# Dealing rows to partitions in consecutive blocks in a hash-attention and feed-forward kernel

## The chip, the cores and the metric

The kernel runs on one core of a Trainium2 chip. The metric is device time in microseconds (us) of the whole program; lower is better. The core has the matrix engine TensorE (PE in the profile, its weight loads PEld), VectorE (DVE), ScalarE (ACT), GpSimd (POOL) and SyncE (SP), which here only issues DMAs. SBUF and PSUM, the on-chip memories, have 128 partitions.

## The reference

Two operations follow each other. The first is attention in which a query sees only the keys whose hash bucket is its own: six sign bits of a projection make the bucket.

```python
B, H, S, D = 4, 8, 768, 64
q_bits = (np.einsum('bhsd,dk->bhsk', q, proj) > 0)      # proj: 64 x 6
k_bits = (np.einsum('bhsd,dk->bhsk', k, proj) > 0)
mask = q_bucket[:, :, :, None] == k_bucket[:, :, None, :]
scores = np.where(mask, np.matmul(q, k.transpose(0, 1, 3, 2)) / 8, -1e9)
attn = softmax(scores)                                  # with 1e-9 added to the sum
x = (attn @ v).transpose(0, 2, 1, 3).reshape(B, S, 512)
# the second: layer norm without a bias, and a feed-forward layer added to x
xn = (x - x.mean(-1)) / np.sqrt(x.var(-1) + 1e-6) * g_ln
out = x + np.maximum(xn @ w_ch1, 0.0) @ w_ch2           # 512 -> 2048 -> 512
```

Inputs and output are float32. The kernel multiplies in bfloat16, the hash bits aside, which come from float32 matmuls.

## The kernel before

**Tiling.** The work is cut into 12 units u: batch b = u // 3, and a third of the query rows, 256 of 768, in two tiles of 128. A unit has six steps s, two groups g of four heads by three key pieces kp of 256 keys. Step s computes transposed scores (`scores`, L182), their exponential (`exps`, L189, ScalarE), and one step later the product with v (`av`, L206). After three steps `normalize` (L219 to L223) divides by the row sums and collects statistics; after six `center` (L230 to L233) subtracts the mean, and `flip` (L238) transposes the result by DMA. Then come `ff1` (L248, relu at L252 into `hb`), `ff2` (L258, residual at L265 into `res`) and `store` (L272), spread over the following unit's steps.

**How rows sit on partitions.** The 768 rows of a head are tt = 32 blocks of 24 neighbouring rows; a block is c = 4 times kj = 6 rows. q and k of four heads are loaded with (head, tt) on the partitions, so a partition holds 24 neighbouring rows of one head. VectorE then transposes blocks of 32x32, which puts a row's 64 features on the partitions (two halves j of 32) and tt in the free dimension. `turn` (L78 to L83, batches 1 to 3, three kj at a time) and `first_piece` (L282 to L288, batch 0, two kj at a time) lay the columns out in the order (kj, c, tt): the 32 values of a block are neighbours in memory. A matmul over 128 columns then takes one kj, and its partition is p = 32 c + tt. For that v must have the same order: partition 32 c + tt takes the rows 24 tt + 6 c to 24 tt + 6 c + 5. One DRAM view holds this for only one c, so `load_v` (L145) issues four DMAs of 32 partitions per half of the heads, and `store` (L272) four per unit.

**Hash.** For batch 0, `first` transposes one piece, casts it, multiplies by the projection (L301) and takes the signs (`bits`, L86) into G, one piece after another. For batches 1 to 3, `turn_piece` (four per tensor and group, 16 per batch), `cast_full` (GpSimd, L97 and L113), `hash_mm` (L123) and `bits` (L86) do the same in larger pieces; then `hash_move` (L133) issues 16 small DMAs per group.

**Order.** Every piece of work is an event with a key in units of steps, and the program is emitted in the order of the keys; each engine works through its own list in that order. q and k of the next batch are transposed in the seven steps ahead of their first use (S0 = 18 b + 3 g):

```python
at(S0 - 7 + 1.3 * t + 0.3 * n, turn_piece, b, g, t, n)
at(S0 - 5.7 + 1.3 * t, cast_full, b, g, t)
at(S0 - 4.2, hash_mm, b, g)
at(S0 - 3.9 + 0.1 * (4 * c + i), hash_move, b, g, c, i)
at(S0 - 9, load_v, b, 0)
at(6 * u + 6.12, flip, u)
```

Nearly all DMAs are issued by SyncE (q, k, v, w_ch1, hash moves, flips, stores), so that its list is one queue: a flip stands behind the hash moves and stores with smaller keys. Buffers shared by name tag set further waits: three for X (the loaded q and k), two for `big` (v and the pieces of w_ch1 in turn), one PSUM buffer each for `f1`, `f2`, `acc` and `sc`. In batch 0 the pieces of w_ch1 are cast on VectorE (`cast_w1`, L316) between the pieces of `first`, and the v sums (`sum_v`, L164 to L166) are taken on GpSimd.

Of the kernel before, what the change touches and what calls it, by code (L numbers as in the profile page):

```python
# [15 lines left out]
def kernel(  # L16
# [15 lines left out]
    nc = tc.nc  # L32
    P = 128
    B, H, S, D = q.shape
# [5 lines left out]
    KJ, CC, TT = 6, 4, 32  # L40
# [9 lines left out]
    def qk_view(t, b, g):  # L50
        return t[b, 4 * g : 4 * g + 4].rearrange("i (tt r) d -> (i tt) (r d)", tt=TT)

    v_view = [v[b].rearrange("h (tt c kj) d -> c tt h (kj d)", tt=TT, c=CC) for b in range(B)]
    out_view = [out[b].rearrange("(tt c u qt) d -> u c tt (qt d)", tt=TT, c=CC, u=3) for b in range(B)]
    w1ap = moe_w_ch1.rearrange("(o p) h -> p o h", p=P)
    w2ap = moe_w_ch2.rearrange("(o p) d -> p o d", p=P)

# [16 lines left out]
    X, T, vnat = {}, {}, {}  # L74
    sc, E, acc = {}, {}, {}
    xt, stats, rstd, xc, xnT, hb, f2, res = {}, {}, {}, {}, {}, {}, {}, {}


    def turn(dst, src, j, kj0, n):

        s = src.rearrange("p (c kj j dd) -> p j kj c dd", c=CC, j=2, dd=32)
        d = dst.rearrange("p j (kj c t) -> p j kj c t", c=CC, t=32)
        nc.vector.transpose(d[:, j, kj0 : kj0 + n], s[:, j, kj0 : kj0 + n])  # L83

    def bits(dst, src):
# [7 lines left out]
    def cast_q(eng, b, g, src, lo, hi):  # L93
        if eng is nc.scalar:
            nc.scalar.activation(qb[b, g][:, :, lo:hi], src, AF.Copy, scale=QS)
        else:
            eng.tensor_scalar(qb[b, g][:, :, lo:hi], src, QS, None, op0=AOP.mult)  # L97
# [5 lines left out]
    def turn_piece(b, g, t, n):  # L103
        if n == 0:
            T[b, g, t] = pool.tile([P, 2, S], F32, name=f"T{b}{g}{t}", tag="T", bufs=2)
        j, half = n // 2, n % 2
        turn(T[b, g, t], X[b, g, t], j, 3 * half, 3)
# [31 lines left out]
    def load_v(b, hs):  # L139
        if hs == 0:  # L140
            vnat[b] = pool.tile([P, H, KJ * D], F32, name=f"vnat{b}", tag="big", bufs=2)
            vaug[b] = pool.tile([P, H, KJ, D + 1], BF16, name=f"vaug{b}", tag="vaug", bufs=2)
            vsum[b] = pool.tile([P, H, D + 1], BF16, name=f"vsum{b}", tag="vsum", bufs=2)
        for c in range(CC):
            nc.sync.dma_start(  # L145
                out=vnat[b][32 * c : 32 * c + 32, hs : hs + 4],
                in_=v_view[b][c][:, hs : hs + 4],
            )

    def cast_v(b, hs, n):  # L150
        nc.gpsimd.tensor_copy(
# [116 lines left out]
            )  # L268

    def store(u):  # L270
        for c in range(CC):
            nc.sync.dma_start(  # L272
                out=out_view[u // 3][u % 3][c],
                in_=res[u][32 * c : 32 * c + 32].rearrange("p t d -> p (t d)"),
            )


    def x_piece(b, g, t, kp, tag, bufs, eng):
# [4 lines left out]
    def first_piece(b, g, t, kp, tag, bufs, caster):  # L283
        tp = pool.tile([P, 2, 256], F32, name=f"T{b}{g}{t}{kp}", tag=tag, bufs=bufs)
        for j in range(2):
            s = X[b, g, t, kp].rearrange("p c (kj j dd) -> p j kj c dd", j=2, dd=32)
            d = tp.rearrange("p j (kj c t) -> p j kj c t", c=CC, t=32)
            nc.vector.transpose(d[:, j], s[:, j])  # L288
        lo, hi = 256 * kp, 256 * kp + 256
        if t == 0:  # L290
            cast_q(caster, b, g, tp, lo, hi)
        elif caster is nc.scalar:
            nc.scalar.copy(kb[b, g][:, :, lo:hi], tp)
        else:
            caster.tensor_copy(kb[b, g][:, :, lo:hi], tp)
        return tp
# [7 lines left out]
    def first(g, t, kp, xtag, ttag, caster, bank):  # L304
        tp = first_piece(0, g, t, kp, ttag[0], ttag[1], caster)
        first_hash(0, g, t, kp, tp, bank)
# [20 lines left out]
    def start_loads():  # L327
        nc.vector.memset(pfull, 0.0)
        nc.vector.memset(warm, 0.25)
        x_piece(0, 0, 0, 0, *XP, nc.sync)  # L330
        x_piece(0, 0, 1, 0, *KX, nc.sync)
        for i in range(4):
            nc.scalar.dma_start(
                out=pfull[32 * i : 32 * i + 32, :, 32 * i : 32 * i + NB],
                in_=proj.rearrange("(j dd) n -> dd j n", j=2),
            )
        nc.scalar.dma_start(out=g_sb, in_=moe_g_ln.rearrange("(o p) -> p o", p=P))
        nc.vector.memset(bias_sb, EXP_BIAS)
        nc.gpsimd.memset(p32, 0.0)
        nc.gpsimd.memset(mhalf, -0.5)  # L340
        nc.gpsimd.memset(epsm, EPS_ROW)
        for kp in (1, 2):
            x_piece(0, 0, 1, kp, *KX, nc.sync)
        load_v(0, 0)
        for i in range(4):
            nc.gpsimd.tensor_copy(
                p32[32 * i : 32 * i + 32, :, 8 * i : 8 * i + NB],
                pfull[32 * i : 32 * i + 32, :, 32 * i : 32 * i + NB],
            )
# [16 lines left out]
    for kp in range(3):  # L366
        at(-0.5 + 0.1 * kp, x_piece, 0, 1, 1, kp, *KX, nc.sync)
    at(-0.3, load_v, 0, 4)
    at(-0.2, cast_v, 0, 0, 4)
    at(0.6, sum_v, 0, 0, 4)  # L370
# [23 lines left out]
    for b in range(1, B):  # L394
        for g in range(2):
            S0 = 18 * b + 3 * g
            at(S0 - 10, load_x, b, g, 0)
            at(S0 - 9.5, load_x, b, g, 1)
            at(S0 - 7.2, new_group, b, g)
            for t in range(2):  # L400
                for n in range(4):
# [3 lines that stand above are left out]
            for c in range(4):  # L405
                for i in range(4):
                    at(S0 - 3.9 + 0.1 * (4 * c + i), hash_move, b, g, c, i)
        S0 = 18 * b
        at(S0 - 9, load_v, b, 0)
        at(S0 - 8.8, load_v, b, 4)  # L410
        at(S0 - 5, ones_v, b)
        for hs in range(0, 8, 2):
            at(S0 - 5 + 0.5 * hs / 2 + (2.6 if hs > 3 else 0), cast_v, b, hs, 2)
        for hs in (0, 4):
            at(S0 - 3.2 + 2.6 * hs / 4, sum_v, b, hs, 4)
# [22 lines left out]
    for u in range(NU):  # L438
        for p in range(4):
            ff(ff1, u, p, "f1" if u or p % 2 == 0 else "f2")  # L440
            if u:
                key = ff(ff2, u - 1, 1, p, "f2")
                if p == 3:
                    at(key + 0.3, store, u - 1)
            else:
                chunk[0] += 1
        ff(ff1, u, 4, "f1")
        ff(ff1, u, 5, "f2")
        ff(ff1, u, 6, "f1")
        ff(ff2, u, 0, 0, "f2")  # L450
        ff(ff1, u, 7, "f1")
        for p in range(1, 4):
            ff(ff2, u, 0, p, "f2")
    for p in range(4):
        key = ff(ff2, NU - 1, 1, p, "f1")
    at(key + 0.3, store, NU - 1)

    with tc.manual_schedule():
# [32 lines left out]
```

The softmax here doesn't subtract the row's maximum and nothing guards it: scores larger than these inputs give would overflow.

## Time and profile before

| | us |
|---|---|
| runs of the kernel before, median of three | 366.18 |
| lowest and highest | 364.65, 366.58 |
| span of the profiled execution, first to last instruction | 363.9 |
| first unit's preparation, until the feed-forward begins | about 64 |

The profiled execution has no recorded time of its own beside its span. What a run's time has beyond the span lies ahead of the first and behind the last instruction.

| operation | count | mean us | busy us |
|---|---|---|---|
| block transpose L288, 128x256 f32, VectorE | 24 | 0.419 | 9.1 |
| block transpose L83, 128x384 f32, VectorE | 48 | 0.555 | 25.4 |
| relu L252, VectorE | 96 | 0.683 | 65.6 |
| hash matmul L301, 128x256 f32, TensorE | 48 | 0.514 | 18.1 |
| v load L145, issue on SyncE, 192 KB each | 32 | 0.436 (median) | |
| store L272, issue on SyncE, 128 KB each | 48 | 0.418 (median) | |
| hash move L133, issue on SyncE | 96 | 0.721 (median) | |

A pair or run of transposes overlaps a little: in the start two of them take 0.76 us together, and in a run of L83 they begin 0.48 us apart.

In the profile's rows a line number is one of the listing above. A row of waits gives who waited for whom, the sum in us, how often, and the longest. A row of the chain gives a start time, a length, and the engine with its work; the chain runs back from the last instruction of the program through whatever released each step. A row of engines gives busy us, share of the span and number of instructions. The rows of digits cut the span into 40 slices and give tenths of busy time.

### The profile page before, as it was taken

What the parts mean: (1) busy time and instruction counts of PE and PEld (TensorE: products, weight loads), DVE (VectorE), ACT (ScalarE), POOL (GpSimd) and SP (SyncE); (2) the same over time, 40 slices, a digit from 0 to 9 for tenths busy, and PEclk for the clock granted to TensorE, in tenths of its full rate; (3) what the DMA queues carried; (4) which work ended last, traced back from release to release, by engine and by line L of the source; (5) the groups of instructions that cost most, each with busy time, mean ns of one, the idle gap of its engine ahead of it and who ended that gap; (6) DMA issues with size and microseconds to landing.
All of it is one profiled execution on the core that took longest, in us unless ns stands there. A gap on an engine that the chain in (4) does not pass through costs nothing.

```text
span 363.9 us, 9678 instructions
## 1 busy us (share of the span) xinstructions
PE 312.7 (86%) x4281; PEld 209.8 (58%) x4344; DVE 183.3 (50%) x373; ACT 144.7 (40%) x76; POOL 100.5 (28%) x106
## 2 busy tenths in 40 slices
PE   8674457989988989989989989898889899897993
PEld 3353335766665666756656657666656567565561
DVE  1427245385662363578444534955624545446341
ACT  2344204662453554445246445533535455442000
POOL 1656142019940010069710010399200100101000
PEclk9989555899999999999999999999999999999899
DMA  7799931991021039860030279700210302203022
GB/s 170 174 243 212 306 112 29 273 260 23 9 64 34 3 88 278 193 141 7 12 78 13 59 204 242 192 7 8 64 35 2 88 2 59 31 2 78 10 59 58
DMA packets 34873, 35.68 MB, mean 98 GB/s; under 512 B 17424, under 2 KB 29712, under 8 KB 34832
## 3 DMA queue, kind: packets, MB, share of 16 engines
q1 hardware_dynamic: 31872, 32.96, 36.0%
q0 software_dynamic: 2112, 2.10, 3.6%
q8 instruction: 34, 0.56, 0.6%
q10 hardware_dynamic: 848, 0.01, 0.2%
q14 instruction: 7, 0.06, 0.1%
HBM read 27.27 MB, written 6.29 MB: 92 GB/s over the span
## 4 chain that ended last, share of the span: by engine, by line
PE 66%; DVE 15%; SPq 5%; DMA 4%; issue 3%; ACT 3%; POOL 1%; ACTq 0%; DVEq 0%; POOLq 0%
PE f L248 19%; PE f L258 18%; PE sc L182 11%; PE acc L206 8%; PE hf L301 4%; SPq L133 4%; DVE hb L252 3%; ACT E L189 3%; PE hp L123 2%; DVE xc L231 2%; DMA w1f<-in_moe_w_ch_dram 2%; DMA xnT<-xc 2%; PE warm L354 2%; DVE x L221 2%; DVE st L223 1%
## 5 line engine op out<-in xcount | busy, mean ns | idle before, releaser
L189 ACT ACTIVATE E<-sc,bias_sb 128x2048 bf16<-128x2048 f32 x72 | 141.6, 1967 | 173.9 <-PE sc L182 173.9
L248 PE MATMUL f<-xnT,w_sb 128*128 128x256 bf16 x768 | 99.7, 274 | 16.3 <-DVE hb L252 13.8
L248 PEld LDWEIGHTS <-w_sb 128*128 128x128 bf16 x768 | 72.4, 98 | 39.1 <-issue 23.0
L252 DVE TENSOR_SCALAR hb<-f 128x512 bf16<-128x512 f32 x96 | 65.6, 683 | 52.7 <-PE f L248 51.4
L258 PE MATMUL f<-w_sb,hb 128*128 128x512 bf16 x321 | 86.9, 385 | 3.5
L232 POOL TENSOR_SCALAR rs<-mv 128x2 f32<-128x2 f32 x12 | 6.1, 512 | 199.6 <-DVE mv L230 199.6
L182 PE MATMUL sc<-qb,kb 32*128 32x256 bf16 x1152 | 54.2, 275 | 0.0
L258 PEld LDWEIGHTS <-hb 128*128 128x128 bf16 x384 | 35.2, 99 | 30.5 <-issue 3.2
L206 PEld LDWEIGHTS <-E 128*128 128x128 bf16 x1152 | 43.1, 100 | 11.4 <-issue 10.5
L206 PE MATMUL acc<-vaug,E 128*128 128x65 bf16 x1152 | 49.5, 198 | 0.0
L265 DVE SCALAR_TENSOR_TENSOR res<-f,rs,x 128x512 f32<-128x512 f32 x24 | 18.0, 751 | 54.7 <-PE f L258 50.7
L182 PE MATMUL sc<-G 6*128 6x256 bf16 x576 | 41.9, 280 | 4.0 <-ACT E L189 3.9
L97 POOL TENSOR_SCALAR qb<-T 128x1536 bf16<-128x1536 f32 (+1 forms) x10 | 30.6, 3059 | 13.4 <-DVE T L288 13.4
L182 PEld LDWEIGHTS <-G 6*128 6x128 bf16 x576 | 15.4, 92 | 29.7 <-issue 28.6
L182 PEld LDWEIGHTS <-kb 32*128 32x128 bf16 x1152 | 30.8, 96 | 2.0
L301 PE MATMUL hf<-T,pfull 128*128 128x256 f32 x48 | 18.1, 514 | 13.6 <-DVE T L288 13.5
L83 DVE STREAM_TRANSPOSE T<-X 128x384 f32<-128x384 f32 x48 | 25.4, 555 | 0.0
L301 PEld LDWEIGHTS hf<-T,pfull 128*128 128x128 f32 x48 | 10.7, 246 | 18.7 <-DVE T L288 17.2
L223 DVE BATCH_NORM_STATS2 st<-x 128x6 f32<-128x256 f32 x48 | 18.1, 418 | 0.8
L221 DVE TENSOR_TENSOR x<-acc,rc 128x512 f32<-128x512 f32 x24 | 16.6, 692 | 0.8
L86 DVE TENSOR_SCALAR G<-hf 128x256 bf16<-128x256 f32 x12 | 5.1, 425 | 23.5 <-PE hf L301 23.5
L219 DVE RECIPROCAL rc<-acc 128x8 f32<-128x8 f32 x24 | 4.9, 205 | 21.1 <-PE acc L206 21.1
(35 smaller groups left out, 147.9 us busy)
## 6 DMA issues: line engine op xcount, KB each, us to landing
vnat<-in_v_dram SPq DMA_DIRECT2D x32, 192.0 KB
out_dram<-res SPq DMA_DIRECT2D x48, 128.0 KB
X<-in_q_dram SPq DMA_DIRECT2D x6, 768.0 KB
X<-in_k_dram SPq DMA_DIRECT2D x6, 768.0 KB
w1f<-in_moe_w_ch_dram SPq DMA_DIRECT2D x4, 1024.0 KB
w_sb<-in_moe_w_ch_dram POOLq DMA_DIRECT2D x4, 512.0 KB, 8.5
X<-in_q_dram SPq DMA_DIRECT2D x6, 256.0 KB
X<-in_k_dram SPq DMA_DIRECT2D x6, 256.0 KB
```

Source lines behind the costliest of these rows:

```text
L83: nc.vector.transpose(d[:, j, kj0 : kj0 + n], s[:, j, kj0 : kj0 + n])
L97: eng.tensor_scalar(qb[b, g][:, :, lo:hi], src, QS, None, op0=AOP.mult)
L182: nc.tensor.matmul(sc[s][:, i, 256 * kk : 256 * kk + 256], lh, rh, start=(rep == 0), stop=(rep == 2), skip_group_check=True,)
L189: nc.scalar.activation(E[s], sc[s], AF.Exp, scale=EXP_SCALE, bias=bias_sb)
L206: nc.tensor.matmul(acc[u, g][:, qt, (D + 1) * i : (D + 1) * (i + 1)], E[s][:, i, 256 * kk + P * qt : 256 * kk + P * qt + P], vaug[u // 3][ ...
L221: nc.vector.tensor_tensor(xo, a[:, :, :, 0:D], rc.to_broadcast([P, 2, 4, D]), op=AOP.mult)
L223: nc.vector.bn_stats(stats[u][:, qt, g], xt[u][:, qt, 256 * g : 256 * g + 256])
L248: nc.tensor.matmul(f1[:, n].rearrange("p (t x) -> p t x", t=2), w1_sb[:, dt, P * nt : P * nt + P], xnT[u][:, :, dt], start=(dt == 0), stop ...
L252: nc.vector.tensor_scalar_max(hb[u][:, 2 * p : 2 * p + 2], f1, 0.0)
L258: nc.tensor.matmul(f2[u, t], hb[u][:, nt, P * t : P * t + P], w2_sb[:, nt], start=(nt == 0), stop=(nt == NNT - 1),)
L265: nc.vector.scalar_tensor_tensor(res[u][:, t], f2[u, t], rstd[u][:, t : t + 1], xt[u][:, t], op0=AOP.mult, op1=AOP.add,)
L301: nc.tensor.matmul(hp[:, :256], pfull[:, j], tp[:, j], start=(j == 0), stop=(j == 1))
```

## The change

Partition p now takes the rows 6 p to 6 p + 5, that is p = 4 tt + c where it was 32 c + tt. v and the output then have one regular view over all 128 partitions, and the four DMAs become one. The transposes of q and k have to deliver their columns in the same order, (kj, tt, c): the 32 values of a block are written four elements (16 bytes) apart, and the four blocks of one kj interleave. Nothing else is edited; the readers of the transposed tiles still read them without gaps.

```diff
-    v_view = [v[b].rearrange("h (tt c kj) d -> c tt h (kj d)", tt=TT, c=CC) for b in range(B)]
-    out_view = [out[b].rearrange("(tt c u qt) d -> u c tt (qt d)", tt=TT, c=CC, u=3) for b in range(B)]
+    v_view = [v[b].rearrange("h (p kj) d -> p h (kj d)", p=P) for b in range(B)]
+    out_view = [out[b].rearrange("(p u qt) d -> u p (qt d)", p=P, u=3) for b in range(B)]
...
     def turn(dst, src, j, kj0, n):
 
         s = src.rearrange("p (c kj j dd) -> p j kj c dd", c=CC, j=2, dd=32)
-        d = dst.rearrange("p j (kj c t) -> p j kj c t", c=CC, t=32)
+        d = dst.rearrange("p j (kj t c) -> p j kj c t", c=CC, t=32)
         nc.vector.transpose(d[:, j, kj0 : kj0 + n], s[:, j, kj0 : kj0 + n])
...
-        for c in range(CC):
-            nc.sync.dma_start(
-                out=vnat[b][32 * c : 32 * c + 32, hs : hs + 4],
-                in_=v_view[b][c][:, hs : hs + 4],
-            )
+        nc.sync.dma_start(out=vnat[b][:, hs : hs + 4], in_=v_view[b][:, hs : hs + 4])
...
     def store(u):
-        for c in range(CC):
-            nc.sync.dma_start(
-                out=out_view[u // 3][u % 3][c],
-                in_=res[u][32 * c : 32 * c + 32].rearrange("p t d -> p (t d)"),
-            )
+        nc.sync.dma_start(out=out_view[u // 3][u % 3], in_=res[u].rearrange("p t d -> p (t d)"))
...
             s = X[b, g, t, kp].rearrange("p c (kj j dd) -> p j kj c dd", j=2, dd=32)
-            d = tp.rearrange("p j (kj c t) -> p j kj c t", c=CC, t=32)
+            d = tp.rearrange("p j (kj t c) -> p j kj c t", c=CC, t=32)
             nc.vector.transpose(d[:, j], s[:, j])
```

## The prediction

> **What bounds the kernel now.** I read the page's busy shares first, then its forty slices, then the waits of TensorE, and last the chain of work at the places where the edited instructions stand.
>
> ```profile
> PE 312.7 (86%) x4281; PEld 209.8 (58%) x4344; DVE 183.3 (50%) x373; ACT 144.7 (40%) x76; POOL 100.5 (28%) x106
> PE   8674457989988989989989989898889899897993
> ...
> DVE  1427245385662363578444534955624545446341
> ```
>
> From about 64 us on TensorE is busy nine tenths of the time, so a delay there costs only if TensorE waits for it. Before 64 us no engine is full: that stretch is a ladder of short dependences. VectorE is half busy on average, but 8 or 9 tenths in the slices near 73, 164 and 228 us, where the next batch's block transposes are squeezed in.
>
> ```profile
> PE f L248 <- DVE hb L252: 13.8, 11, 2.1
> PE hf L301 <- DVE T L288: 13.5, 8, 5.8
> PE acc L195 <- POOL vsum L166: 4.2, 2, 2.6
> PE sc L182 <- ACT E L189: 3.9, 5, 1.1
> PE hp L123 <- DVE hb L252: 2.4, 3, 0.8
> PE f L248 <- DMA xnT<-xc: 2.3, 2, 1.3
> ```
>
> These are TensorE's waits (total us, times, longest). The largest two are for VectorE: in the start for a transpose (L288), later for the relu `hb` (L252), and what holds `hb` up is seen in the chain at 152 us:
>
> ```profile
> 151.70 0.75 DVE res L265
> 152.45 0.48 DVE T L83
> 152.93 0.57 DVE hb L252
> 153.51 0.48 DVE T L83
> 153.99 0.58 DVE hb L252
> 154.56 0.48 DVE T L83
> ...
> 157.93 0.61 DVE hb L252
> 158.54 0.04 issue
> 158.59 1.03 PE f L248 x8
> ```
>
> VectorE runs without a gap for 7 us, three transposes are links of it, and TensorE waits 1.2 us at its end. The waits for `xnT` (2.3 us) are the only ones that the SyncE queue causes: the batch turnover's 32 hash moves (L133) and a store (L272) stand ahead of the flip (L238).
>
> [...] 128x384 takes 555 ns and 128x256 takes 419, so (555 - 419)/128 = 1.06 ns per column. It shows no strided write. [...] while X and v are loaded (64 to 84 us) the DMA engines are 94% busy.
>
> **The transposes.** Their counts, shapes and reads stay; each write steps by 16 bytes. I price a column at 2.1 ns[...]. Added per instruction: 256 x 1.05 = 0.27 us (L288, 24 of them), 384 x 1.05 = 0.40 us (L83, 48 of them); VectorE's busy time grows by 6.5 + 19.2 = 25.7 us. [...] A gain is excluded: no write gets shorter.
>
> *In the start* the chain passes nine pairs of L288, near 10, 12, 14, 23, 30, 36, 46, 50 and 53 us. The hash matmul begins after the first of a pair, so usually the first alone shows: at 10, 12, 23 and 30 us the hash takes 1.15 us, its half of 0.57 covers the second (which ends 0.34 + 0.27 + 0.69 = 1.30 us after the pair's start; the half ends at 0.42 + 0.27 + 0.04 + 0.57 = 1.30), giving 4 x 0.27. At 46, 50 and 53 us the hash takes 2.09 us and covers more, 3 x 0.27. At 14 us a cast on GpSimd and at 36 us a reload of X wait for both, and behind them come the v sums and the w1f load on which the chain goes on: 2 x 0.54. Sum 1.08 + 0.81 + 1.08 = 3.0 us (1.9 at the low price; 4.5 at the high one, where the second transpose shows 0.1 four times).
>
> *At each of three turnovers* (work for batches 1, 2, 3; I follow the second, 150 to 177 us):
> - 152 to 158 us: three links, 3 x 0.40 = 1.2 us. The first turnover has two and a crowded pair ahead of them, and comes to nearly as much.
> - 158.5 to 161 us: four more transposes before the hash matmul L123 at 162.06. The last ended at 160.99, so the slack was 1.07; they add 4 x 0.40 = 1.6, so TensorE waits 0.6.
> - 166.4 to 176 us: VectorE must finish `hb` before the next ff1 matmuls can have their one bank. Three transposes add 1.2 against 0.48 of idle time, so a relu that ended 0.17 before TensorE came for it ends about 0.6 after. Then four add 1.6 against 0.73 of slack beyond the 0.6 already lost; after the last relu the hash at 175.7 is about 1.2 late in all.
>
> Together 1.2 + 0.6 + 1.2 = 3.0, three times 9.0 us. At the low price the middle wait vanishes and the last is 0.3, so 3 x 1.1 = 3.2; at the high price 1.7 + 1.2 + 2.3 = 5.2, so 15.6. Waiting behind a longer transpose are `hb`, the normalization and center on VectorE; TensorE waits for them.
>
> **The v loads.** 32 issues (median 0.436 us) become 8; the bytes and, going by contiguous runs of 1536 B, the packets stay. I cost this at nothing: it frees SyncE of some 10 us, but its only waits there are for X transfers ahead of it, GpSimd's one wait for v is 1.0 us, and at 64 to 84 us transfers, not issues, are the limit. If the cover went, 1.0 us would be at stake, either way.
>
> **The stores.** 48 issues become 12, each turn 1.7 us less some 0.43. At the turnovers this moves the flip 1.3 us earlier; the waits for `xnT` (1.1 and 1.3 us, first and third turnover) go: -2.4. Next late there is TensorE itself, which was busy up to 192 us in the second turnover, where nothing is gained. Elsewhere SyncE is idle behind a store. At the end the result is ready at 359.13, four issues last to 360.87, the span ends at 363.9. One issue saves up to 3 x 0.43 = 1.3 us, but one transfer of 512 KB must then move what had a staggered start, so I take half, -0.6 (bounds 0 and -1.3).
>
> **Sum.** 3.0 + 9.0 - 2.4 - 0.6 = +9.0 us on the profiled span of 363.9, giving 372.9. No separate time of the profiled execution is shown; the runs lie 0.75 to 2.7 us above that span, their median 366.18 is 2.3 above. With the same distance: 366.18 + 9.0, rounded to **375.2**.
>
> **Rivals.**
> 1. *The strided write is free*[...]: only the gains count, -3.0, 363.2. [...] This is the case on the faster side[...].
> 2. *The low price[...]:* 1.9 + 3.2 - 3.0 = +2.1, so 368.3. For it: with less than 0.3 us per transpose most of the slacks named above hold.
> 3. *The high price[...]:* 4.5 + 15.6 - 3.0 = +17.1, so 383.3. [...] In its turnovers VectorE is the bound.
> 4. *The merged DMAs bring nothing, or arrive in one lump and later:* then the gain of 3.0 is missing, 378.2. For it: the same bytes on engines already 94% busy. Against: the gains I count are issue time on SyncE, not bandwidth.
>
> **Chances.** My forecast (371.5 to 379) 0.41; high price or beyond 0.20; low price (368 to 371.5) 0.17; costs and gains nearly equal (364.4 to 368) 0.10; free write 0.12. Half a per cent, 1.8 us, is about what a measurement of this kernel can tell from no change; so faster 0.12, same 0.10, slower 0.78. The range, 367 to 384.5, leaves out the free write, part of the even case[...].
>
> **What would show it.** The means of L288 and L83 decide: 0.69 and 0.96 us for my price[...], unchanged for the free write. TensorE's wait for the transpose in the start should grow by about 2 us, those for `hb` and before L123 by about 9 together, and those for `xnT` should vanish. L272 should show 12 issues and L145 eight, with SyncE's stretch from the last result to the end shorter by up to 1.3 us. I am wrong if the transposes slow down but TensorE's waits don't grow (slack that I missed, or work reordered by the delay), or if v arrives later and GpSimd's sums hold up TensorE.

## The result, and the profile after

The changed kernel takes **371.01 us** (median of four runs, 369.19 to 372.63) against 366.18: a ratio of 1.0128, 95% interval 1.0088 to 1.0169. Measured again beside the last experiments, 22 runs gave a median of 369.26 against 365.40 of the kernel before, 3.9 us more. Without the seven slowest of the 22, which lie more than 1.5% above the fastest, the median is 367.66 and the ratio 1.0050 (1.0019 to 1.0082), some 2 us; falls of the clock that come with the change (below) may have made these runs slow, so both figures are given. The change makes the kernel slower by 2 to 5 us, half of the forecast of 9 or less. The profiled execution took 369.19 us with a span of 367.4: 1.8 us lie around the span.

First what the transposes cost now. The first line is from the page: busy us, share of the span and count of each engine. The other two are from the groups by shape: busy us, mean ns of one, idle time before them.

```profile
PE 319.6 (87%) x4344; PEld 211.3 (58%) x4344; DVE 198.7 (54%) x373; ACT 144.7 (39%) x76; POOL 100.4 (27%) x106
```

```profile
L83 DVE STREAM_TRANSPOSE T<-X 128x384 f32<-128x384 f32 x48 | 38.7, 860 | 0.0
...
L280 DVE STREAM_TRANSPOSE T<-X 128x256 f32<-128x256 f32 x24 | 13.0, 614 | 2.4 <-DMA X<-in_q_dram 2.4
```

The same 72 instructions take 0.305 and 0.195 us more each. The slope between the shapes is (860 - 614)/128 = 1.92 ns per column, where it was 1.06. VectorE's busy time grew by only 15.4 us, since neighbouring instructions overlap: 0.21 us for each of the 72.

TensorE's waits in the changed kernel, in total us, times and longest:

```profile
PE f L244 <- DVE hb L248: 15.5, 11, 2.0
PE hf L293 <- DVE T L280: 15.3, 8, 6.6
...
PE hp L123 <- DVE hb L248: 2.4, 3, 0.8
...
PE f L244 <- DMA xnT<-xc: 0.4, 1, 0.4
```

The waits for `hb` rose by 1.7 us, not by 9; those for the first transposes by 1.8 (over the thirteen profiles of these runs they are 14.3 to 16.2 us where the start has strided writes and 12.7 to 15.3 where it has not); the wait ahead of L123 is what it was; those for `xnT` are nearly gone. The chain at the second turnover, for comparison with the one shown before:

```profile
154.46 0.78 DVE T L83
155.24 0.52 DVE hb L248
155.76 0.75 DVE T L83
156.51 0.52 DVE hb L248
157.03 0.77 DVE T L83
...
157.86 0.70 DVE x L217
...
160.61 0.61 DVE hb L248
161.22 0.04 issue
161.26 1.03 PE f L244 x8
```

Each of the three links is 0.3 us longer. But TensorE's wait at its end grew from 1.18 to 1.84 us, by 0.66 and not by 0.9. The rest is lost in overlap: VectorE's next instruction begins 0.15 us before the record of a strided transpose ends, where it was 0.08, so the `hb` links are 0.05 shorter. In the kernel before, the multiplication behind the third transpose stands in the chain as

```profile
155.18 0.70 DVE x L221
```

From the start of the first transpose to this one it was 155.18 - 152.45 = 2.73 us and is now 157.86 - 154.46 = 3.40: a transpose delays what comes after it by 0.22 us, though its own record grew by 0.305.

**Where the time went, stage by stage.** The 72 exponentials are a ruler: both kernels have them in the same order. The table gives how much later than in the kernel before one stretch of them passes, from one profile each. The three turnovers are exponentials 10 to 17, 31 to 35 and 49 to 53; the waits for `xnT` follow each; the end is what comes after the last exponential.

| profile of | start | turnover 1 | xnT | turnover 2 | xnT | turnover 3 | xnT | end | sum |
|---|---|---|---|---|---|---|---|---|---|
| changed kernel | 2.4 | 0.66 | -1.1 | 1.0 | -0.2 | 2.6 | -0.9 | -1.0 | 3.5 |
| changed kernel, again | 1.4 | 0.66 | -1.1 | 2.6 | -0.2 | 2.6 | -1.1 | -1.0 | 3.9 |
| strided writes alone | 1.0 | 0.66 | 0.0 | 2.6 | 0.0 | 2.6 | 0.0 | 0.0 | 6.9 |
| strided writes in the turnovers alone, DMAs merged | 1.3 | 0.64 | -1.1 | 2.6 | -0.2 | 2.6 | -1.2 | -1.0 | 3.7 |
| merged DMAs alone | 2.4 | 0.0 | -0.9 | 0.0 | -0.2 | 0.0 | -1.3 | -2.7 | -2.7 |
| changed kernel, four transposes earlier | 2.7 | 0.3 | -1.1 | 0.4 | -0.2 | 0.3 | -1.0 | -1.0 | 0.4 |

From the tenth exponential on, the columns repeat to some 0.2 us (the last `xnT` to 0.4), with two exceptions: in the second and third turnover strided writes cost either 1.0 or 2.6, and the end is -1.0 or -2.7. The start doesn't repeat: over thirteen profiles it lies between -1.0 and +2.8 us, with or without strided writes. Its cost can be read only from medians of many runs.

**The 1.6 us between 1.0 and 2.6** are a fall of TensorE's clock. These rows of the changed kernel give, for the 5 us after the two long waits, the busy us of PE, PEld, DVE, ACT and POOL with the number of instructions in brackets; the number after the last bracket is the granted clock, then the DMA share and GB/s.

```profile
161.00:166.00 5.00, 4.74 (x66) 3.08 (x65) 3.69 (x6) 0.50 (x1) 5.00 (x5) 1.00 0.58 82
238.00:243.00 5.00, 4.86 (x34) 3.05 (x33) 3.52 (x6) 0.36 (x1) 5.00 (x5) 0.66 0.31 73
```

The same stretch of the program follows both waits. After the first it runs at full clock, after the second at a mean of 0.66, and TensorE gets through half as many matmuls (34 against 66) in the same 5 us. The wait and the eight matmuls behind it, in the order kernel before, then changed kernel:

```profile
158.59 1.03 PE L248 MATMUL f<-xnT,w_sb 128*128 128x256 bf16 x8 [1.18 <-DVE hb L252]
...
234.64 1.03 PE L248 MATMUL f<-xnT,w_sb 128*128 128x256 bf16 x8 [1.17 <-DVE hb L252]
```

```profile
161.26 1.03 PE L244 MATMUL f<-xnT,w_sb 128*128 128x256 bf16 x8 [1.84 <-DVE hb L248]
...
238.14 1.86 PE L244 MATMUL f<-xnT,w_sb 128*128 128x256 bf16 x8 [1.86 <-DVE hb L248]
```

Waits of 1.24 us or less before, of 1.84 and 1.86 here. In the four profiles with strided writes in their usual places in the turnovers, eight waits of 1.84 to 1.86 us occur in turnovers 2 and 3, and seven of them are followed by slower matmuls. None of the waits of 1.17 to 1.57 us at this place is.

The waits can be set against the clock's own times. In the profiles of the two kernels the clock changes only at edges that lie a multiple of 3.41 us apart, and every fall between the start and the last store is one such step at 0.50: from 336.40 us in the kernel before, from 238.09 and 340.49 in the changed kernel. The first row of the changed kernel is the step in which most of the spared wait lies, the others are the step of the second wait and the two behind it:

```profile
159.59:163.00 3.41, 1.74 (x27) 1.56 (x27) 3.38 (x7) 1.91 (x1) 2.74 (x3) 1.00 1.00 229
234.68:238.09 3.41, 1.60 (x28) 0.82 (x27) 3.25 (x10) 2.27 (x2) 0.95 (x2) 1.00 0.66 211
238.09:241.51 3.42, 3.37 (x27) 2.46 (x27) 3.42 (x5) 0.28 (x1) 3.42 (x2) 0.50 0.44 98
241.51:244.92 3.41, 3.41 (x54) 1.85 (x56) 0.22 (x2) 0.00 (x0) 3.41 (x6) 1.00 0.02 5
```

The spared wait, 159.42 to 161.26, is cut by the edge at 159.59; the other, 236.28 to 238.14, lies in one step but for 0.05 us. Behind the start the two profiles have two more waits of 1.84 us or more, both of 2.05 us at the last unit: 333.07 to 335.12 in the kernel before and 337.59 to 339.64 in the changed one. Each lies whole in a step (from 332.99 and from 337.07), and a step at half clock follows. Of these four waits the three that lie in one step are followed by a fall, and the one that is cut is not. A shorter wait of 1.56 us that lies whole in a step (82.64 to 84.20 in the changed kernel, in the step from 81.08) is spared. These are few cases, and no run moved a wait against the edges on purpose. That the wait is the reason is an inference from where the falls stand; what shortens the wait was tried (last experiment but one), and the falls in the turnovers were gone.

### The profile page after: what moved, and what is told of

Its sections match the earlier page's. It is cut to its first block, busy times and chain, and to the rows that moved or that the text cites. A ratio compares the mean times of both kernels' runs of the same rounds, so it can differ in the third digit from the quotient of the medians.

```text
span 367.4 us, 9645 instructions
## 1 busy us (share of the span) xinstructions
PE 319.6 (87%) x4344; PEld 211.3 (58%) x4344; DVE 198.7 (54%) x373; ACT 144.7 (39%) x76; POOL 100.4 (27%) x106
## 4 chain that ended last, share of the span: by engine, by line
PE 65%; DVE 24%; DMA 3%; ACT 3%; issue 3%; POOL 1%; SPq 0%; ACTq 0%; DVEq 0%; POOLq 0%
PE f L244 18%; PE f L254 18%; PE sc L178 11%; PE acc L202 8%; DVE T L83 5%; DVE hb L248 5%; PE hf L293 4%; DVE xc L227 3%; DVE x L217 3%; ACT E L185 3%; PE hp L123 2%; DMA w1f<-in_moe_w_ch_dram 2%; DVE st L219 2%; PE warm L346 2%; DVE T L280 2%
## 5 line engine op out<-in xcount | busy, mean ns | idle before, releaser
L244 PE MATMUL f<-xnT,w_sb 128*128 128x256 bf16 x768 | 100.5, 275 | 16.2 <-DVE hb L248 15.5
L254 PE MATMUL f<-w_sb,hb 128*128 128x512 bf16 x384 | 97.4, 384 | 0.1
L202 PEld LDWEIGHTS <-E 128*128 128x128 bf16 x1152 | 44.0, 101 | 11.6 <-issue 10.5
L202 PE MATMUL acc<-vaug,E 128*128 128x65 bf16 x1152 | 50.3, 199 | 0.0
L83 DVE STREAM_TRANSPOSE T<-X 128x384 f32<-128x384 f32 x48 | 38.7, 860 | 0.0
L97 POOL TENSOR_SCALAR qb<-T 128x1536 bf16<-128x1536 f32 (+1 forms) x10 | 30.6, 3059 | 15.4 <-DVE T L280 13.9
L293 PE MATMUL hf<-T,pfull 128*128 128x256 f32 x48 | 18.1, 513 | 15.3 <-DVE T L280 15.3
```

What stands on the lines that cost most here:

```text
L202: nc.tensor.matmul(acc[u, g][:, qt, (D + 1) * i : (D + 1) * (i + 1)], E[s][:, i, 256 * kk + P * qt : 256 * kk + P * qt + P], vaug[u // 3][ ...
L244: nc.tensor.matmul(f1[:, n].rearrange("p (t x) -> p t x", t=2), w1_sb[:, dt, P * nt : P * nt + P], xnT[u][:, :, dt], start=(dt == 0), stop ...
L254: nc.tensor.matmul(f2[u, t], hb[u][:, nt, P * t : P * t + P], w2_sb[:, nt], start=(nt == 0), stop=(nt == NNT - 1),)
L293: nc.tensor.matmul(hp[:, :256], pfull[:, j], tp[:, j], start=(j == 0), stop=(j == 1))
```

## The experiments

In several kernels the columns and the rows of v or the output no longer match; their work, and so their time, is that of the kernels they come from.

**1. The merged DMAs alone**, twice. The two lines of the transposes' patterns are put back.

```diff
-        d = dst.rearrange("p j (kj t c) -> p j kj c t", c=CC, t=32)
+        d = dst.rearrange("p j (kj c t) -> p j kj c t", c=CC, t=32)
...
-            d = tp.rearrange("p j (kj t c) -> p j kj c t", c=CC, t=32)
+            d = tp.rearrange("p j (kj c t) -> p j kj c t", c=CC, t=32)
```

> The merged v loads and stores alone: transposes write without gaps, in the column order of before, while v and the output follow the new one, so that this kernel pairs queries, keys and v of different rows; the amount of work is the same. Theory (strided writes cost, merged stores save): the two waits for xnT go (2.0 us) and the end is 1.0 us shorter, so about 366.2 - 3.0 = 363.2, with transposes at 0.42 and 0.555 us. Rival 1 (the merged DMAs bring nothing, the shift of the waits was chance): 366.2. Rival 2 (the merged loads bring v and X later and make the loss): 368 or more.

> The merged DMAs alone once more (gapless transposes, columns and rows don't match up), to have the price of the strides within one set. Theory: 362.5, ratio 0.990; the changed kernel less this one is 8 us, of which 2.4 in the start, 4.2 without and up to 6 with falls of the clock in the turnovers. Rival (v merged costs about 1 us, as its run alone suggested): ratio 0.993 to 0.995.

Measured: 362.37 us against 365.61 (ratio 0.9901, 0.9863 to 0.9940), and 362.34 against 365.40 (0.9878, 0.9822 to 0.9934). So the merging saves a little over 3 us, as the theory says, and rivals 1 and 2 of the first text fall, as does the one of the second. In the first profile's table row the end is 2.7 us shorter and not 1.0: the rest is again the clock, which fell at the last long wait (2.05 us, near 335 us) in the kernel before and not in this one: over 334 to 338 and 338 to 342 us it was 0.80 and 0.77 before and 1.00 here.

**2. The strided writes alone.** The same two lines, in the other direction, in the kernel before.

> The strided writes alone, with the four v loads and four stores of before, so that columns and rows don't match up; the amount of work is the same. Theory: the start grows by 2.4 us, the three turnovers by 2.2 us (0.7 each) plus about 2 us if TensorE's clock falls back in one of them, no gain: 370.8 to 373. Rival 1 (no gain from DMAs): as after, about 371.0. Rival 2 (the loss came with the loads): 366 to 367.

Measured: 372.86 us against 365.61 (ratio 1.0157, 1.0104 to 1.0210; six runs, 368.46 to 375.22), within the range expected. The rival that blames the loads falls. The waits for `xnT` are there as before, and their columns in the table are zero.

**3. The strides in the start alone, and in the turnovers alone**, each with merged DMAs: one of the two lines put back.

> Merged DMAs, strided writes only in the 24 transposes of batch 0, gapless ones in batches 1 to 3, whose columns then don't match the rows of v and the output. Theory: 363.2 + 2.4 = 365.6. Rival 1: 366.2 + 2.4 = 368.6. Rival 3 (the start's delay is absorbed by the wait for w1f, and the loss is all in the turnovers): 363.2.

> Merged DMAs, strided writes only in the 48 transposes of batches 1 to 3; the columns of batch 0 don't match the rows of v and the output. Theory: 363.2 + 3 x 0.7 = 365.3 without a fall of TensorE's clock in a turnover, 367.3 with one. Rival 1: 368.3 and more. Rival 3 (all the loss is here): 371.

Measured: 364.76 us (ratio 0.9955, 0.9931 to 0.9979) and 366.19 us (1.0007, 0.9985 to 1.0028), both against 365.61. Over the 362.37 of the merged DMAs alone, the start's strides cost 2.4 us and the turnovers' 3.8. Together 6.2, where the changed kernel is 369.26 - 362.34 = 6.9 above, or 5.3 with its other median, 367.66 (8 was expected): the parts add up to within what such medians tell. Rival 1, with 368 and more, falls, and so does rival 3, that the start absorbs its part.

**4. Which merging saves.** Gapless transposes and one of the two DMAs in four parts again:

```diff
-        nc.sync.dma_start(out=vnat[b][:, hs : hs + 4], in_=v_view[b][:, hs : hs + 4])
+        for c in range(CC):
+            nc.sync.dma_start(
+                out=vnat[b][32 * c : 32 * c + 32, hs : hs + 4],
+                in_=v_view[b][32 * c : 32 * c + 32, hs : hs + 4],
+            )
```

> Gapless transposes, v merged, stores in four parts of 32 partitions of the new view; columns and rows don't match up as in the run of the merged DMAs alone. Theory (v brings nothing): 366.2, with waits for xnT of about 2 us. Rival (v loads brought part of the gain): 364 to 365.

> Gapless transposes, stores merged, v in four parts of 32 partitions; columns and rows don't match up. Theory: the whole gain, 363.2; waits for xnT near zero. Rival (v loads brought part of the gain): 364.5 to 365.5.

Measured: v merged 366.45 us against 364.99 (ratio 1.0034, 1.0009 to 1.0060); stores merged 362.45 (0.9946, 0.9921 to 0.9970). The saving is the stores': in the profile with stores merged `xnT` and the end are shorter by 1.1, 1.1 and 1.0 us, as in the table. v merged alone came out slightly slower than the kernel before. Its profile can't explain that, being of the fastest of the 22 runs (363.17 us), and with both merged no such loss is seen (experiment 1). This stays open.

**5. The price by itself.** Eight transposes of one kind in a row, a kind per line, and DMAs with nothing beside them.

```python
for _ in range(N):      # L69: the change's pattern, 128x384; L71 the same, 128x256
    nc.vector.transpose(Ti.rearrange("p (kj t c) -> p kj c t", c=CC, t=32), s[:, 0, 0:3])
for _ in range(N):      # L75, L77, L79, L81, L83: steps of 2, 3, 4, 8, 24 words
    nc.vector.transpose(T4[:, :, 0], f)
```

> Only transposes and DMAs, each kind by itself; nothing of the reference is computed. Theory: a 128x384 transpose takes 0.555 us gapless and at a stride of 2 words[...], about 0.86 at 4 words in the kernel's pattern and at 4, 8 and 24 words alike, (0.86 - 0.62)/128 = 1.9 ns per column. Rival: the cost grows with the stride[...]. For the DMAs: a v tile of 768 KB in one DMA lands sooner than in four of 32 partitions by at least the three issues (1.3 us); rival: by far more[...].

Measured, as groups by shape (busy us, mean ns; L67 and L73 write without gaps):

```profile
L83 DVE STREAM_TRANSPOSE T<-X 128x384 f32<-128x384 f32 x8 | 9.1, 1133 | 0.2
L81 DVE STREAM_TRANSPOSE T<-X 128x384 f32<-128x384 f32 x8 | 6.9, 863 | 0.2
L69 DVE STREAM_TRANSPOSE Ti<-X 128x384 f32<-128x384 f32 x8 | 6.8, 852 | 0.2
L79 DVE STREAM_TRANSPOSE T<-X 128x384 f32<-128x384 f32 x8 | 6.8, 846 | 0.2
L77 DVE STREAM_TRANSPOSE T<-X 128x384 f32<-128x384 f32 x8 | 5.4, 679 | 0.2
...
L75 DVE STREAM_TRANSPOSE T<-X 128x384 f32<-128x384 f32 x8 | 4.6, 574 | 0.2
L73 DVE STREAM_TRANSPOSE Tc<-X 128x384 f32<-128x384 f32 x8 | 4.6, 573 | 0.2
```

Two words apart cost nothing (574 ns against 573), three 0.11 us, four and eight the same 0.27 to 0.29 us, and 24 words twice that, 0.56. Over the 1.06 ns of a gapless column, four words are (846 - 574)/384 = 0.71 ns more, 1.77 in all, and 24 words 1.46 more, 2.5. Neither theory nor rival had both: the cost does not grow from four to eight words, but it does to 24. Why it takes this course no run shows.

For the DMAs, the chip's timeline of one v tile in one DMA and then in four (start, length; the copy that follows waits for the landing):

```profile
65.84 0.39 SPq L85 DMA_DIRECT2D V<-in_v_dram  x1
70.39 0.17 DVE L86 COPY probe<-V 128x4 f32<-128x4 f32 x1 [4.58 <-DMA V<-in_v_dram]
70.59 1.74 SPq L88 DMA_DIRECT2D V<-in_v_dram  x4
76.27 0.17 DVE L89 COPY probe<-V 128x4 f32<-128x4 f32 x1 [5.70 <-DMA V<-in_v_dram]
```

4.6 against 5.7 us: 1.1 less (0.9 and 0.8 in the two pairs that followed), no more than the three issues that are gone (1.74 - 0.39 = 1.35), so not by far more, and the rival falls. A 512 KB store is likewise seen to end after 3.0 us instead of 3.9, and this 0.9 is nearly the 1.0 us at the changed kernel's end.

**6. The new order made by the loads.** q and k are loaded so that gapless transposes give the new order. Batch 0 keeps its runs of 512 B; later loads have runs of 1536 B where they had 6144, and every load becomes four. The patterns of the transposes are those of the kernel before; the loads of batch 0 (`x_piece`) are split in the same way.

```diff
-        nc.sync.dma_start(out=X[b, g, t], in_=qk_view((q, k)[t], b, g))
+        for i in range(4):   # qk_head: t[b, h], rows as "(c tt kj) d -> tt c (kj d)"
+            nc.sync.dma_start(
+                out=X[b, g, t][32 * i : 32 * i + 32].rearrange("p (c x) -> p c x", c=CC),
+                in_=qk_head((q, k)[t], b, 4 * g + i),
+            )
```

> The new row order made by the loads of q and k instead of the transposes: partition tt takes rows 6 (32 c + tt) and following for each c, in four DMAs of 32 partitions per tile, whose runs are 1536 B (512 B in batch 0, as before); v and stores merged, all writes gapless. Theory: the saving of the merged stores without the cost of the strides, 363.2, if the loads of q and k stay hidden; issues on SyncE are 72 more. Rival 1: smaller runs and more issues bring X late in the start and the turnovers, 368 or more. Rival 2: no change from before, 366.

Measured: 363.81 us against 364.99 (ratio 0.9959, 0.9934 to 0.9985). Rival 1 falls, and rival 2 narrowly. The theory's saving of 3.0 us is not reached: 1.2 us were measured, and the merged stores alone saved 2.5 in the same set (362.45 in experiment 4). So the split loads seem to give back about 1 us; by itself such a load takes 5.5 to 5.8 us where one DMA takes 4.5 to 4.7 (the kernel of experiment 5). Where the loss lies in this kernel is not shown. This version computes the same result as both kernels and is faster than both.

**7. The first four transposes of a batch earlier.** Strided writes as in the changed kernel; only the place is another.

```diff
-            at(S0 - 7.2, new_group, b, g)
+            at(S0 - 8.3, new_group, b, g)
...
-                    at(S0 - 7 + 1.3 * t + 0.3 * n, turn_piece, b, g, t, n)
+                    at(S0 - (7 if g or t else 8.2) + 1.3 * t + 0.3 * n, turn_piece, b, g, t, n)
```

> The changed kernel once more, beside the others of this set. Theory: 371 against 366 before, ratio 1.013; the spread of its runs is larger than that of the kernel before, if TensorE's clock falls back in some turnovers of some runs.

> The changed kernel with the first four transposes of each batch emitted 1.2 steps earlier, so that they fall into VectorE's gaps of 0.7 to 1.8 us and not into its gapless run of 7 us. Theory (in a turnover the strides cost because three of them are links of that run, and the long wait lets the clock fall): the run is 2.3 us shorter, TensorE's waits for hb go down by about 4 us, and 366 to 367 is reached; strided writes keep 0.86 us each. Rival (VectorE's total work is what costs): no change from 371. Rival (X isn't there so early): VectorE waits for X, and it gets slower.

Measured: the changed kernel 369.26, and with earlier transposes 364.28 us (ratio 0.9962, 0.9938 to 0.9986, against 365.40). So 5.0 us come back, or 3.4 from the other median of the changed kernel, without a nanosecond off the transposes, which still take 0.86 us; the rival of total work falls, and VectorE didn't wait for X. The expected 366 to 367 was too cautious, and the gapless run of 7 us had set the end by only 0.66 of the 1.84 us that TensorE waited. In this kernel's timeline of VectorE, the four now fall where it was idle:

```profile
147.50 0.86 DVE L83 STREAM_TRANSPOSE T<-X 128x384 f32<-128x384 f32 x1
148.96 0.69 DVE L248 TENSOR_SCALAR hb<-f 128x512 bf16<-128x512 f32 x1 [0.60 <-PE f L244]
149.57 2.24 DVE L83 STREAM_TRANSPOSE T<-X 128x384 f32<-128x384 f32 x3
```

and TensorE's wait in the turnover is the 1.17 us of every unit, with the matmuls behind it at their full 1.03:

```profile
160.53 1.03 PE L244 MATMUL f<-xnT,w_sb 128*128 128x256 bf16 x8 [1.17 <-DVE hb L248]
```

This 1.17 us is what the product with v leaves. In a unit without a transpose, here of the kernel before, the normalization starts when that product is done:

```profile
182.71 0.21 DVE L219 RECIPROCAL rc<-acc 128x8 f32<-128x8 f32 x1 [0.68 <-PE acc L206]
```

The reciprocal begins 0.05 us after the product's last matmul here (182.66). In the second turnover of that kernel, behind the third transpose, it begins 0.07 us after it (154.97 for 154.90): the gapless transposes were out of the way just in time.

**8. Both together.** The loads of experiment 6 and the places of 7.

> The row order made by the loads of q and k (gapless transposes, v and stores merged), with the first four transposes of each batch 1.2 steps earlier. Theory: 363.8 of the read-side kernel less three times the 1.2 us that TensorE waits for VectorE's gapless run: 360 to 361. Rival (X not there yet in the first turnover): 364 or more.

Measured: 363.50 us against 365.40 (ratio 0.9941, 0.9916 to 0.9966). Faster than both kernels, but not the 360 to 361 that I expected, and not told apart from experiment 6. The expectation took the 1.2 us wait for `hb` to come from the transposes; it stayed, 13.8 us in all as before, for with gapless writes the product with v ends no earlier than they do.

## Why the prediction was half right

**The direction and its reasons hold.** Strided writes slow the transposes, some of that reaches TensorE in the start and in the turnovers, and the merged stores give back less. Rival 1, the free write, fell by the transposes' durations, 0.305 and 0.195 us longer; rival 4 by experiment 1. The prices in my forecast and in rivals 2 and 3 were assumptions of mine: the kernel before has no strided write to read one from. The time lies between my forecast and rival 2. By mechanism rival 2, the low price, was the nearer: its 1.1 us per turnover is about what showed, and what took the time above its 368.3 is a cost that no case had, the falls of the clock. That the total still came near half of my forecast is luck.

- **The price** was assumed at 2.1 ns per column; 1.77 by itself and 1.92 by slope in the kernel were measured. 0.40 and 0.27 us more per transpose became 0.305 and 0.195.
- **The start**, 3.0 us, came to 2.4 by medians (experiment 3). At the price measured, my eleven links of about 0.2 would give 2.2: the step stands by its sum, though not shown link by link.
- **The turnovers**, 9.0 us, are the step that failed, and the term in it is the cost of a link. First "three links, 1.2 us": 0.66 showed. I added the growth of an instruction's own duration, 0.40 by my price and 0.305 as measured; what counts is how much later the next instruction starts, and that is 0.22. Second, the wait ahead of L123, 0.6, didn't appear: four transposes added 1.03 us to the slack of 1.07 that I had read, not 1.6, and ended just in time (164.69 for a hash at 164.73). Third, the second half of a turnover cost 0.33, not 1.2: three transposes used up the 0.48 of idle time and came 0.15 later, and the next three added 0.70 where I had read 0.73 of slack. As far as these figures tell, the slacks were read about rightly. Sum: 0.66 + 1.0 + 1.0 = 2.7 us, without falls of the clock.
- **The falls of the clock**, 1.6 us each, were missing. One or two of them in a profile bring the turnovers to 4.2 to 5.9, and the medians of experiment 3 to 3.8. They fit the wide scatter of the changed kernel, whose 22 runs go from 364.42 at a mean clock of 0.953 to 372.86 at 0.922 and correlate with it at -0.95, but are not all of it: a step at half clock takes 0.5 x 3.41 / 367 = 0.005 off the mean, so the 0.031 between these two runs are more than six steps, and two turnovers and the last unit have three. The rest would lie in the start: in nine profiles the mean over the first 64 to 66 us is 0.73 to 0.80.
- **The waits for `xnT`**, -2.4: measured -2.1 to -2.6.
- **The end**, -0.6: -1.0. I took half of the three issues; a store alone shows 0.9 of 1.3.
- **v at nothing**: the packets of 512 B to 2 KB are 12,288 in the profiles of both kernels, and the estimate held as far as the sum with the stores goes; alone it is open.

So the sum, in parts as measured: 2.4 + 3.8 - 2.4 - 1.0 = +2.8, where some 2 to 4.8 were measured; what remains is no more than the medians scatter.

## What to carry to other kernels

Price a slower instruction by how much later the next one starts, not by its own duration, and set that against the slack. To see what removing it would gain, look for the same wait in a stretch where it doesn't occur (1.17 us here against 1.18): a chain of last releasers doesn't show the path that ends second, and experiment 8 failed on that. Before a layout change is given up for its price, move the dearer instructions into gaps of their engine; here that alone turned a loss of 2 to 5 us into a gain of 1. A four-byte write every 16 bytes had a price of its own on VectorE, 0.27 us in a 128x384 transpose by itself, and reordering on the load side did without it: 363.81 us against 364.99.

## What the runs showed of the hardware that I had not expected

- TensorE's granted clock fell to 0.50 for one step of 3.41 us after waits of 1.84 to 2.06 us in the midst of busy work: in 7 of 8 cases after 1.84 to 1.86 us in a turnover, in 8 of 11 profiles after 2.05 to 2.06 us at the last unit, and not after 1.57 us or less in a turnover. In the profiles of the two kernels the spared one of four such waits is the one cut by an edge of the 3.41 us steps. A fall in a turnover cost 1.6 us.
- A transpose's cost by step of its write is no smooth curve: 574, 679, 846, 863 and 1133 ns for steps of 2, 3, 4, 8 and 24 words.
- Four DMAs of 32 partitions lost no more than their three further issues (1.35 us) against one of 128: 0.8 to 1.1 us of 5.4 to 5.7 for 768 KB.
